# A new order of TensorE's attention part, and the half-used eighth pass of the third expert's layer 1 for four column blocks at once in 64-row halves

## The chip, the core and the metric

One core of a Trainium2 chip runs the kernel. The metric is the device time of one execution in microseconds (us). The engines of the core that appear below are TensorE (PE in the profile, its weight loads PEld), VectorE (DVE), ScalarE (ACT), GpSimd (POOL) and the DMA queue that SyncE issues (SP).

## The reference

Three layers in a row: an mLSTM attention (2 sequences, 8 heads, 768 tokens, head size 40), a dense mixture of 4 experts over the 1536 tokens of width 320, and a routed mixture of 8 experts of which each token takes one.

```python
# attention, per batch, head, token t
C = f_stab * C + i_stab * outer(v_t, k_t);  n = f_stab * n + i_stab * k_t
y_t = sigmoid(o_t) * (C @ q_t) / max(|n . q_t|, 1)
# first mixture: all 4 experts on all tokens, D = 320, F = 1024
out += p[:, e:e+1] * (relu(x @ w1[e]) @ w2[e])
# second mixture: expert = argmax(x @ w_gate); at most 384 tokens each
out[i] = gate_w[i] * (relu(x[i] @ w1[e]) @ w2[e])
```

The weights come as f32 and are used as pairs of f16 numbers (a high and a low part), so one f32 product is three f16 products.

## The kernel before

The attention is computed in 12 **units** of 128 tokens (2 sequences x 6 chunks). `front(u)` loads a unit, turns q and k by DMA transposes (line 1039), computes the scores (TensorE, line 1119, 8 matmuls), multiplies them by the decay mask on VectorE (line 1163, two halves), splits the product on ScalarE (line 1176) and GpSimd (line 1180) into a high and a low half, and `back(u)` uses both: TensorE's lines 1205 and 1210 (24 matmuls in the unit's second step), the update of the state (line 1273), then the output of the unit, which a DMA transpose (line 632) turns into `xT`, the input of the experts. `xT[:, t]` has five chunks of 128 rows for one tile of 128 tokens: width 320 is two and a half chunks, and chunk 2 holds the last 64 rows of the high part and the last 64 of the low part.

The experts are numbered 0 to 3 (first mixture) and 4 to 11 (second). Layer 1 of a tile (`tile_ops`) is two quads of four column blocks; each block takes 8 passes, listed in `L1_PAIRS` (line 635) as (high or low weights, chunk of the weights, chunk of `xT`). The last, (1, 2, 2), multiplies the low part of the weights' chunk 2 with `xT`'s chunk 2, where only the 64 high rows matter. A PSUM bank of a quad is evacuated by ScalarE (line 663, relu, high half) and VectorE (line 665, low half). Layer 2 of a tile is two halves of 12 matmuls (line 656); its bank is added to `acc` by VectorE (line 697).

Experts 0 and 1 run tile by tile between the attention's units. TensorE's order there is a table written by hand, `SEQ` (line 508): ("S", u) is the scores of unit u, ("B", u) its second part, ("L", k, t) layer 1 of expert k on tile t, ("M", k, t) its layer 2. Due times of all other engines and queues come from it: `Sched` lets every engine take the ready instruction whose result is due first. Where it estimates that TensorE would stand idle in the first part, it puts dummy matmuls (`warm`, line 416). Experts 2 and 3 run afterwards in groups of four tiles, 512 columns (`group_ops`, line 719). PSUM has eight banks; layer 1 takes them in turn from `hring` (there `ph0, ph1, x2, x1`), layer 2 from `oring` (there `po0, po1, x3, x0`).

Each weight matrix gets its scale from its largest magnitude: ScalarE and VectorE reduce it, GpSimd reduces over partitions (line 545), and a one-column matmul of TensorE spreads the scale over the partitions (line 551, a **spread**), placed in TensorE's order by `SPREAD_AT`. While the third expert runs, the weights of experts 8 to 11 and 4 are prepared in this way.

Of the kernel before, what the change touches and what calls it, by code (L numbers as in the profile page):

```python
# [10 lines left out]
F16 = mybir.dt.float16  # L11
# [238 lines left out]
def xlstm_moe_kernel(ctx: ExitStack, tc: tile.TileContext, a, cap: int):  # L250
# [467 lines left out]

    def group_ops(k, t0, nt, at, tail=None):
        wb, n = wbuf[at_work[k]], nt * 128  # L720
        for f in range(NF):
            kp = ps_tile("h")
            ph = bank[kp][:, 0:n]
            ph3 = ph.rearrange("p (t n) -> p t n", t=nt)
            add(
                "PE", 8 * n / 2400.0 + 0.02,
                lambda f=f, ph3=ph3: l1_mm(ph3, wb, f, lambda c: xT[:, t0:t0 + nt, c]),
                [("xT", t0 + j) for j in range(nt)] + w_keys(at_work[k], 1), [kp], at + 0.01 * f,
            )
            evac_ops(ph, kp, hb[0][:, f, 0:n], hb[1][:, f, 0:n], ("bh", f), ("bl", f), ["hbfree"])  # L730
# [1296 lines left out]
```

## Time and profile before

| | before |
|---|---|
| median of 3 runs, us | 496.05 (494.47 to 496.36) |
| profiled execution, us | 495.52 |
| its span in the profile, us | 493.8 |
| mean granted TensorE clock | 0.998 |
| PE, DVE, ACT, POOL busy, us | 475.5, 340.6, 311.9, 131.7 |
| first mixture and attention, third expert, fourth expert, second mixture, us from the span's start | 0 to 233.4, 233.4 to 312.8, 312.8 to 400, 400 to 493.8 |

The profile shows one execution. Busy time is what an engine worked; a matmul's shown end is modelled, so steps from one start to the next are more exact than durations. A wait is the idle time of an engine ahead of an instruction, with what ended it. TensorE's granted clock is written as a part of full speed.

### The profile page before, as it was taken

How to read it: one execution, taken by the hardware profiler on the slowest of the kernel's cores; microseconds unless marked ns; L12 is line 12 of the kernel's file. 1: busy time of each engine (PE TensorE's matmuls, PEld its weight loads, DVE VectorE, ACT ScalarE, POOL GpSimd, SP SyncE). 2: the span in 40 equal slices, each digit the busy share in tenths (PEclk: the TensorE clock that was granted, in tenths of full speed). 3: DMA queues.
4: the chain of work that ended last, by engine and by line, in shares of the span. 5: the costliest groups of instructions: out<-in, count | busy, mean ns of one | idle time of the engine just before them, and what ended most of it. 6: DMA issues, size and time to landing. Idle time of an engine off the chain costs nothing. (4 is left out here: it accounts for less than half of the span.)

```text
span 493.8 us, 13708 instructions
## 1 busy us (share of the span) xinstructions
PE 475.5 (96%) x5487; PEld 365.7 (74%) x5487; DVE 340.6 (69%) x972; ACT 311.9 (63%) x666; POOL 131.7 (27%) x243
## 2 busy tenths in 40 slices
PE   8999999999989899999999999999999999999994
PEld 6998978868868797886564746556564698888883
DVE  5898988799999834663968594879899982222120
ACT  1997979577687854856765568778879550322230
POOL 4751143665865410200010010000414111311111
PEclk9999999999999999999999999999999999999999
DMA  6996683354533796818686967628293545999200
GB/s 229 315 236 195 155 286 77 77 131 102 105 60 73 201 342 205 230 26 288 204 296 220 333 215 298 211 75 222 70 223 109 133 184 79 302 219 322 103 27 25
DMA packets 70772, 88.90 MB, mean 180 GB/s; under 512 B 48641, under 2 KB 56307, under 8 KB 70702
## 3 DMA queue, kind: packets, MB, share of 16 engines
q1 hardware_dynamic: 69502, 84.23, 59.4%
q0 software_dynamic: 1200, 3.73, 2.0%
q8 instruction: 45, 0.74, 0.6%
q14 instruction: 25, 0.20, 0.2%
HBM read 55.89 MB, written 21.70 MB: 157 GB/s over the span
## 5 line engine op out<-in xcount | busy, mean ns | idle before, releaser
L656 PEld LDWEIGHTS <-arena 128*128 128x128 f16 (+1 forms) x1416 | 136.4, 98 | 55.0 <-issue 3.2
L644 PEld LDWEIGHTS <-w 128*128 128x128 f16 x1792 | 97.3, 98 | 4.2 <-issue 2.8
L644 PE MATMUL ph<-xT,w 128*128 128x128 f16 (+3 forms) x1664 | 96.2, 217 | 1.2 <-DVE usm L442 0.9
L644 PEld LDWEIGHTS <-arena 128*128 128x128 f16 x960 | 64.2, 98 | 42.9 <-issue 1.8
L656 PE MATMUL po<-w,arena 128*128 128x320 f16 (+1 forms) x600 | 86.3, 299 | 2.1 <-DVE acc L697 1.3
L527 ACT ACTIVATE junk<-raw 128x512 bf16<-128x512 f32 (+1 forms) x105 | 69.6, 663 | 12.3 <-DMA raw<-in_moe_w_dram 10.8
L656 PE MATMUL po<-arena 128*128 128x320 f16 x504 | 71.3, 299 | 0.4 <-ACT arena L589 0.4
L665 DVE SCALAR_TENSOR_TENSOR arena<-ph,arena 128x512 f16<-128x512 f32 x80 | 54.5, 683 | 22.7 <-ACT arena L663 22.6
L644 PE MATMUL ph<-xT,arena 128*128 128x512 f16 (+4 forms) x512 | 66.7, 284 | 0.0
L589 ACT ACTIVATE w<-raw,wsm 128x640 f16<-128x640 f32 (+1 forms) x56 | 51.3, 961 | 18.1 <-DVE wsm L447 18.0
L663 ACT ACTIVATE arena<-ph 128x512 f16<-128x512 f32 x80 | 47.0, 587 | 22.7 <-PE ph L644 13.4
L594 DVE SCALAR_TENSOR_TENSOR w<-raw,wsm,w 128x640 f16<-128x640 f32 (+1 forms) x56 | 57.4, 1049 | 3.8 <-ACT w L589 3.7
L644 PE MATMUL x<-xT,arena 128*128 128x128 f16 (+4 forms) x448 | 52.2, 270 | 0.0
L545 POOL CROSS_LANE_REDUCE wsm<-wsm 128x1 f32<-128x6 f32 (+1 forms) x24 | 9.6, 402 | 107.9 <-ACT junk L527 78.7
L656 PE MATMUL x<-arena 128*128 128x320 f16 (+1 forms) x240 | 34.6, 299 | 0.1
L594 DVE SCALAR_TENSOR_TENSOR arena<-raw,wsm,arena 128x640 f16<-128x640 f32 (+1 forms) x28 | 30.4, 1103 | 3.0 <-ACT arena L589 3.0
L589 ACT ACTIVATE arena<-raw,wsm 128x640 f16<-128x640 f32 (+1 forms) x28 | 25.5, 955 | 3.6 <-DVE wsm L447 3.6
L685 POOL TENSOR_TENSOR cfs<-pw,invx 128x1 f32<-128x1 f32 x48 | 17.1, 388 | 37.1 <-DVE invx L452 29.8
L697 DVE SCALAR_TENSOR_TENSOR acc<-po,cfs,acc 128x320 f32<-128x320 f32 x30 | 16.4, 546 | 14.0 <-PE po L656 7.5
L1770 POOL DMA_INDIRECT out_dram<-acc,usm x13 | 12.7, 975 | 46.9 <-ACT acc L1767 45.0
L1180 POOL TENSOR_TENSOR arena<-arena 128x512 f16<-128x512 f32 x16 | 20.6, 1304 | 12.0 <-ACT arena L1176 12.0
L1457 POOL DMA_INDIRECT disp<-arena x12 | 13.8, 1150 | 34.5 <-ACT arena L663 17.3
(237 smaller groups left out, 649.3 us busy)
## 6 DMA issues: line engine op xcount, KB each, us to landing
raw<-in_moe_w_dram SPq DMA_DIRECT2D x36, 512.0 KB
raw<-in_moe_w_dram SPq DMA_DIRECT2D x24, 640.0 KB
ws<-w SPq DMA_DIRECT2D x8, 768.0 KB
ws<-w SPq DMA_DIRECT2D x8, 640.0 KB
arena<-in_att_dram SPq DMA_DIRECT2D x8, 492.0 KB
disp<-zero SPq DMA_DIRECT2D x1, 3936.0 KB
arena<-ws SPq DMA_DIRECT2D x4, 768.0 KB
arena<-ws SPq DMA_DIRECT2D x4, 640.0 KB
```

The lines of the kernel that those rows point to most:

```text
L527: nc.scalar.activation(out=junk[:, 0:w], in_=raw[:, i * w:(i + 1) * w], func=AF.Abs, accum_out=am[:, i:i + 1])
L589: lambda sl=sl: nc.scalar.activation(out=wh[:, sl], in_=raw[:, sl], func=AF.Copy, scale=sc),
L594: lambda sl=sl: nc.vector.scalar_tensor_tensor(wl[:, sl], raw[:, sl], sc, wh[:, sl], ALU.mult, ALU.subtract),
L644: nc.tensor.matmul(out=out, lhsT=wb[wi][:, c, f * 128:(f + 1) * 128], rhs=rhs(xc), start=(i == 0), stop=(i == LAST))
L656: nc.tensor.matmul(out=po[0:n, 0:DM], lhsT=hs[:, f, sl], rhs=ws[:, f, :], start=(f == 0 and i == 0), stop=(f == NF - 1 and i == 2),)
L663: act(0.52, lambda: nc.scalar.activation(out=hh, in_=ph, func=AF.Relu), [kp] + ex, [kh])
L665: 0.6, lambda: nc.vector.scalar_tensor_tensor(hl, ph, 0.0, hh, ALU.max, ALU.subtract),
L685: 0.26, lambda: nc.gpsimd.tensor_tensor(cf, pw[:, t, k:k + 1], invx[:, t:t + 1], ALU.mult),
L697: lambda: nc.vector.scalar_tensor_tensor(acc[:, t], po[:, 0:DM], cf, acc[:, t], ALU.mult, ALU.add),
L1180: 1.3, lambda j=j: nc.gpsimd.tensor_tensor(Wl[:, j::2], pb[:, j::2], Wh[:, j::2], ALU.subtract),
L1457: sent[k("done")] = nc.gpsimd.indirect_dma_start(out=disp_t[t], out_offset=bass.IndirectOffsetOnAxis(ap=sli, axis=0), in_=R.bitcast(U32), ...
L1770: nc.gpsimd.indirect_dma_start(out=view_of(), out_offset=bass.IndirectOffsetOnAxis(ap=ix[0:n], axis=0), in_=acc[0:n, y], in_offset=None, b ...
```

## The change

Two things, in one diff. First, another `SEQ`: the same items in another order. Second, the third expert's layer 1 (`group_ops` with `halves`) does 7 passes for each column block, and the eighth pass of four blocks together by `l1_halves_mm`: four matmuls of 64 rows, two on rows 0 to 63 with `xT`'s chunk 2 and two on rows 64 to 127 with `x4`, a copy of `xT`'s 64 high rows that three DMAs place there. The rows 64 to 127 of the weights' chunk 2 hold the same low part as the rows 0 to 63. The evacuations of the four blocks come after all of it, in the order 0, 2, 1, 3. The banks of the stage are dealt otherwise: six for layer 1 (`ph0, ph1, x2, x1, x3, x0`), two for layer 2 (`po0, po1`).

```diff
+    x4 = w2area.take([NT, 128], F16)
...
- ("S", 0), ("B", 0), ("S", 1), ("B", 1), ("L", 0, 0), ("S", 2), ("L", 0, 1), ("M", 0, 1), ("B", 2), ("S", 3), ("L", 0, 2),
+ ("S", 0), ("B", 0), ("S", 1), ("B", 1), ("L", 0, 0), ("L", 0, 1), ("S", 2), ("M", 0, 0), ("B", 2), ("L", 0, 2), ("S", 3),
...
-    def l1_mm(out, wb, f, rhs):
-        for i, (wi, c, xc) in enumerate(L1_PAIRS):
+    def l1_mm(out, wb, f, rhs, n=LAST + 1):
+        for i, (wi, c, xc) in enumerate(L1_PAIRS[:n]):
...
+    def l1_halves_mm(wb, q, out, t0, nt):
+        wi, c, xc = L1_PAIRS[LAST]
+        for y in range(2):
+            for z, x in enumerate((xT[0:64, t0:t0 + nt, xc], x4[64:128, t0:t0 + nt])):
+                f = q + 2 * z + y
+                nc.tensor.matmul(
+                    out=out[2 * z + y], lhsT=wb[wi][64 * z:64 * z + 64, c, f * 128:(f + 1) * 128], rhs=x,
+                    start=False, stop=True,
+                )
...
+            if halves:
+                add(
+                    "PE", 0.62, lambda q=q, ph3=ph3: l1_halves_mm(wb, q, ph3, t0, nt), keys + [("x4", t0)], kps,
+                    at + 0.01 * (q + 3) + 0.005,
+                )
+                for y in (0, 2, 1, 3):
+                    f = q + y
+                    evac_ops(phs[y], kps[y], hb[0][:, f, 0:n], hb[1][:, f, 0:n], ("bh", f), ("bl", f), ["hbfree"])
...
+    for t0 in range(0, NT, 4):
+        dma(
+            x4[64:128, t0:t0 + 4], xT[0:64, t0:t0 + 4, 2], 1.0, ["w2free"] + [("xT", t0 + j) for j in range(4)], [("x4", t0)],
+        )
...
     hring.append("x1")
-    oring.extend(["x3", "x0"])
+    hring.extend(["x3", "x0"])
     for t0 in range(0, NT, 4):
-        group_ops(2, t0, 4, at + 10 + 0.5 * t0)
-    hring.remove("x1")
-    del oring[2:]
+        group_ops(2, t0, 4, at + 10 + 0.5 * t0, None, True)
+    del hring[3:]
```

Counted over the whole program, the instructions differ in three places: 55 dummy matmuls instead of 64 (24 instead of 33 in the stretch from 16 us on), 24 matmuls of 64 rows in place of 24 of 128, and three DMAs more.

What the table does on VectorE can be counted in its order. The first mask multiply of units 4 to 11 stands at these places:

| unit | 4 | 5 | 6 | 7 | 8 | 9 | 10 | 11 |
|---|---|---|---|---|---|---|---|---|
| before | 155 | 198 | 234 | 258 | 296 | 315 | 349 | 373 |
| after | 133 | 171 | 202 | 256 | 288 | 318 | 353 | 369 |

Ahead of layer 1 of expert 0 on tile 3, VectorE's order has 157 instructions before and 190 after. TensorE's own order brings the scores of units 4, 5 and 6 by 7.8, 13.2 and 11.1 us of its work nearer to the start; those of units 7 to 11 move by 2.7 us or less.

**SP's queue**, where the tiles and units change places. Line 1039 (1065 after) is the transpose of a unit's q and k, line 632 (633) that of a unit's output into `xT`, line 422 (423) any other transfer. Before, from the transpose of tile 3 (first row):

```order
L632 DMA_TRANSPOSE xT<-arena 128x5x128
L1039 DMA_TRANSPOSE arena<-arena 128x16x128
L422 DMA arena<-in_att_dram 128x320
L422 DMA arena<-in_att_dram 128x984
L422 DMA arena<-arena 40x328 x2
L632 DMA_TRANSPOSE xT<-arena 128x5x128
L1039 DMA_TRANSPOSE arena<-arena 128x16x128
L422 DMA arena<-in_att_dram 128x984
L422 DMA arena<-in_att_dram 128x320
L1039 DMA_TRANSPOSE arena<-arena 128x16x128
L632 DMA_TRANSPOSE xT<-arena 128x5x128
```

and now, from the transpose of unit 5's q and k (first row):

```order
L1065 DMA_TRANSPOSE arena<-arena 128x16x128
L423 DMA arena<-in_att_dram 128x320
L423 DMA arena<-in_att_dram 128x984
L423 DMA gsm<-gsm 128x1x1
L633 DMA_TRANSPOSE xT<-arena 128x5x128
L423 DMA arena<-arena 40x328 x2
L423 DMA arena<-in_att_dram 128x320
L1065 DMA_TRANSPOSE arena<-arena 128x16x128
L423 DMA arena<-in_att_dram 128x984
L633 DMA_TRANSPOSE xT<-arena 128x5x128
L1065 DMA_TRANSPOSE arena<-arena 128x16x128
L633 DMA_TRANSPOSE xT<-arena 128x5x128
```

The transposes of units 5 and 6 now stand ahead of those of tiles 3 and 4, where they stood behind them; unit 7's stands ahead of tile 5's in both.

**TensorE at the end of a column block of the third expert** (`ph`, `x` and `po` are PSUM banks; `arena` holds weights and the copy `x4`). Before, from the last pass of one block, past the spread of a scale, to the first of the next:

```order
L644 MATMUL ph1_98<-xT_70,arena_88 128x512
L644 LDWEIGHTS arena_88
L644 MATMUL ph1_98<-xT_70,arena_88 128x512
L551 LDWEIGHTS call_68
L551 MATMUL x0_101<-wsm_82,call_68 128x1
```

and now, behind the seventh pass of the fourth block:

```order
L645 MATMUL x3_104<-xT_70,arena_88 128x512
L654 LDWEIGHTS arena_88
L654 MATMUL ph1_98<-xT_70,arena_88 128x512
L654 LDWEIGHTS arena_88
L654 MATMUL x1_102<-arena_88 128x512
L654 LDWEIGHTS arena_88
L654 MATMUL x2_103<-xT_70,arena_88 128x512
L654 LDWEIGHTS arena_88
L654 MATMUL x3_104<-arena_88 128x512
L645 LDWEIGHTS arena_88
L645 MATMUL x0_101<-xT_70,arena_88 128x512
```

Four half-row matmuls to four banks stand between the blocks, two of them with `xT` and two with the copy.

**TensorE at the spread of expert 11's second scale** (`call` is the matrix of ones). Before:

```order
L644 LDWEIGHTS arena_88
L644 MATMUL x2_103<-xT_70,arena_88 128x512
L551 LDWEIGHTS call_68
L551 MATMUL x3_104<-wsm_82,call_68 128x1
L644 LDWEIGHTS arena_88
L644 MATMUL x1_102<-xT_70,arena_88 128x512
```

and now:

```order
L667 LDWEIGHTS arena_88
L667 MATMUL po0_99<-arena_88 128x320
L552 LDWEIGHTS call_68
L552 MATMUL x3_104<-wsm_82,call_68 128x1
L645 LDWEIGHTS arena_88
L645 MATMUL ph0_97<-xT_70,arena_88 128x512
```

The spread stood behind two column blocks of layer 1 (lines 644) of its group; now it stands behind layer 2 of the group before (line 667) and ahead of the first block.

## Rows read from the trace of the kernel before

**Rows 1.** The page, part 1: busy time of each engine.

```profile
PE 475.5 (96%) x5487; PEld 365.7 (74%) x5487; DVE 340.6 (69%) x972; ACT 311.9 (63%) x666; POOL 131.7 (27%) x243
```

**Rows 2.** Windows: stretch, its length, then the engines' busy time, clock, DMA.

```profile
0.00:78.10 78.10, 74.62 (x858) 66.59 (x859) 65.25 (x175) 59.74 (x148) 34.36 (x81) 1.00 0.77 225
40.00:80.00 40.00, 38.53 (x531) 34.13 (x530) 34.28 (x97) 33.23 (x74) 12.53 (x31) 1.00 0.67 191
80.00:100.00 20.00, 19.89 (x291) 16.60 (x288) 16.90 (x55) 13.40 (x30) 8.47 (x17) 1.00 0.45 99
100.00:160.00 60.00, 56.01 (x896) 47.96 (x897) 58.08 (x153) 45.65 (x93) 39.41 (x51) 1.00 0.45 92
160.00:180.00 20.00, 18.73 (x217) 15.45 (x215) 12.82 (x24) 15.29 (x38) 6.49 (x10) 1.00 0.83 249
233.40:312.80 79.40, 77.62 (x474) 45.57 (x472) 59.05 (x107) 51.78 (x95) 5.01 (x12) 1.00 0.73 253
```

**Rows 3.** Waits of TensorE from 40 to 180 us: total, times, longest.

```profile
PE x L1119 <- DMA arena<-arena: 1.3, 2, 1.1
PE po L656 <- DVE acc L697: 1.3, 1, 1.3
PE x L1205 <- ACT arena L1176: 1.1, 1, 1.1
PE ph L644 <- DVE usm L442: 0.9, 1, 0.9
PE po L656 <- DVE arena L665: 0.8, 1, 0.8
```

**Rows 4.** Timeline of unit 7, 109 to 116 us: start, duration, instruction.

```profile
109.32 0.61 PE L1119 MATMUL x<-arena 120*128 120x128 f16 x8
...
111.40 3.74 PE L644 MATMUL ph<-xT,w 128*128 128x128 f16 x64
111.71 1.28 DVE L1163 TENSOR_TENSOR arena<-x,arena 128x512 f32<-128x512 f32 x2
...
112.48 1.23 ACT L1176 ACTIVATE arena<-arena 128x512 f16<-128x512 f32 x2 [0.42 <-DVE arena L1163]
...
113.19 2.65 POOL L1180 TENSOR_TENSOR arena<-arena 128x512 f16<-128x512 f32 x2 [1.08 <-ACT arena L1176]
...
115.19 0.51 PE L1210 MATMUL x<-arena 128*128 128x41 f16 x14
...
115.89 0.42 PE L1210 MATMUL x<-arena 128*128 128x41 f16 x10 [0.20 <-POOL arena L1180]
```

**Rows 5.** Instructions of line 416 from 16 to 45 us, by form.

```profile
L416 PE MATMUL ph<-zero x30: 269/272/282, 27.5 to 41.0; 128*128 128x256 f16 x30
L416 PE MATMUL x<-zero x3: 270/271/274, 16.7 to 16.9; 128*128 128x256 f16 x3
```

**Rows 6.** Timeline of TensorE around a pair of 24-row matmuls.

```profile
84.01 1.66 PE L656 MATMUL po<-w,arena 128*128 128x320 f16 x11
85.60 0.39 PE L1075 MATMUL x<-xT 24*128 24x512 bf16 x2
85.92 0.84 PE L644 MATMUL ph<-xT,w 128*128 128x128 f16 x12
```

**Rows 7.** Timeline of TensorE in the third expert.

```profile
245.44 1.79 PE L656 MATMUL x<-arena 128*128 128x320 f16 x12
247.07 1.79 PE L656 MATMUL po<-arena 128*128 128x320 f16 x12
...
258.60 1.89 PE L644 MATMUL x<-xT,arena 128*128 128x512 f16 x8
260.33 0.17 PE L551 MATMUL po<-wsm,call 128*128 128x1 bf16 x1
```

**Rows 8.** The page, part 5: evacuations of layer 1.

```profile
L665 DVE SCALAR_TENSOR_TENSOR arena<-ph,arena 128x512 f16<-128x512 f32 x80 | 54.5, 683 | 22.7 <-ACT arena L663 22.6
...
L663 ACT ACTIVATE arena<-ph 128x512 f16<-128x512 f32 x80 | 47.0, 587 | 22.7 <-PE ph L644 13.4
```

**Rows 9.** Timeline of TensorE at two spreads of a weight scale.

```profile
288.49 0.16 PE L551 MATMUL x<-wsm,call 128*128 128x1 bf16 x1 [1.07 <-POOL wsm L545]
288.52 1.89 PE L644 MATMUL x<-xT,arena 128*128 128x512 f16 x8
...
307.92 0.16 PE L551 MATMUL x<-wsm,call 128*128 128x1 bf16 x1 [0.71 <-POOL wsm L545]
```

More of the change, by code (lines that the diff above doesn't have):

```diff
@@ L508, in xlstm_moe_kernel @@
     SEQ = {x: i for i, x in enumerate((
- ("S", 0), ("B", 0), ("S", 1), ("B", 1), ("L", 0, 0), ("S", 2), ("L", 0, 1), ("M", 0, 1), ("B", 2), ("S", 3), ("L", 0, 2), ("B", 3), ("M", 0, 0), ("L", 1, 0), ("L", 1, 2), ("M", 1, 0), ("S", 4), ("M", 0, 2), ("L", 1, 1), ("B", 4), ("L", 0, 3), ("M", 1, 2), ("L", 1, 3), ("S", 5), ("L", 0, 4), ("S", 6), ("B", 5), ("M", 0, 4), ("L", 0, 5), ("S", 7), ("B", 6), ("M", 1, 1), ("L", 1, 5), ("B", 7), ("M", 0, 3), ("L", 1, 4), ("S", 8), ("B", 8), ("L", 0, 6), ("M", 0, 5), ("M", 1, 3), ("S", 9), ("B", 9), ("L", 0, 7), ("L", 0, 8), ("L", 1, 6), ("S", 10), ("M", 0, 7), ("L", 1, 9), ("M", 1, 6), ("M", 0, 8), ("M", 0, 6), ("L", 0, 10), ("B", 10), ("L", 0, 9), ("L", 1, 8), ("L", 1, 7), ("M", 0, 10), ("M", 1, 5), ("L", 1, 10), ("S", 11), ("M", 1, 8), ("M", 1, 4), ("B", 11), ("L", 0, 11), ("L", 1, 11), ("M", 1, 7), ("M", 0, 9), ("M", 1, 9), ("M", 1, 10), ("M", 1, 11), ("M", 0, 11),
+ ("S", 0), ("B", 0), ("S", 1), ("B", 1), ("L", 0, 0), ("L", 0, 1), ("S", 2), ("M", 0, 0), ("B", 2), ("L", 0, 2), ("S", 3), ("L", 1, 0), ("B", 3), ("S", 4), ("M", 0, 2), ("M", 1, 0), ("M", 0, 1), ("B", 4), ("L", 1, 1), ("S", 5), ("L", 1, 2), ("L", 1, 3), ("L", 0, 3), ("S", 6), ("B", 5), ("L", 0, 4), ("M", 1, 2), ("B", 6), ("M", 0, 3), ("L", 0, 5), ("M", 1, 1), ("M", 1, 3), ("S", 7), ("L", 1, 5), ("B", 7), ("S", 8), ("M", 0, 4), ("L", 1, 4), ("L", 0, 6), ("B", 8), ("M", 0, 5), ("L", 0, 7), ("S", 9), ("M", 0, 7), ("L", 0, 8), ("L", 1, 6), ("S", 10), ("L", 1, 9), ("M", 0, 6), ("L", 0, 10), ("L", 1, 8), ("L", 1, 7), ("L", 0, 9), ("L", 1, 10), ("M", 1, 7), ("B", 9), ("M", 1, 8), ("M", 1, 6), ("L", 0, 11), ("B", 10), ("M", 0, 9), ("L", 1, 11), ("M", 0, 8), ("M", 1, 5), ("M", 1, 10), ("S", 11), ("M", 1, 4), ("M", 1, 11), ("M", 0, 10), ("B", 11), ("M", 0, 11), ("M", 1, 9),
     ))}
@@ L717, in tile_ops, with group_ops @@
         l2_ops(k, t, wb, hh, hl, 0, [[("hh", i, g), ("hl", i, g)] for g in range(2)], at2)
-    def group_ops(k, t0, nt, at, tail=None):
+    def group_ops(k, t0, nt, at, tail=None, halves=False):
         wb, n = wbuf[at_work[k]], nt * 128
[L721 to L730, printed above, removed]
+        keys = [("xT", t0 + j) for j in range(nt)] + w_keys(at_work[k], 1)
+        for q in range(0, NF, 4):
+            kps, phs, ph3 = [], [], []
+            for f in range(q, q + 4):
+                kp = ps_tile("h")
+                ph = bank[kp][:, 0:n]
+                kps.append(kp)
+                phs.append(ph)
+                ph3.append(ph.rearrange("p (t n) -> p t n", t=nt))
+                passes = LAST if halves else LAST + 1
+                add(
+                    "PE", passes * n / 2400.0 + 0.02,
+                    lambda f=f, out=ph3[-1], passes=passes: l1_mm(out, wb, f, lambda c: xT[:, t0:t0 + nt, c], passes),
+                    keys, [kp], at + 0.01 * f,
+                )
+                if not halves:
+                    evac_ops(ph, kp, hb[0][:, f, 0:n], hb[1][:, f, 0:n], ("bh", f), ("bl", f), ["hbfree"])
+            if halves:
+                add(
+                    "PE", 0.62, lambda q=q, ph3=ph3: l1_halves_mm(wb, q, ph3, t0, nt), keys + [("x4", t0)], kps,
[4 more added lines that the diff above has]
+                    evac_ops(phs[y], kps[y], hb[0][:, f, 0:n], hb[1][:, f, 0:n], ("bh", f), ("bl", f), ["hbfree"])
         for j in range(nt):
@@ L1614, in xlstm_moe_kernel @@
     gate_weights()
+    for t0 in range(0, NT, 4):
+        dma(
+            x4[64:128, t0:t0 + 4], xT[0:64, t0:t0 + 4, 2], 1.0, ["w2free"] + [("xT", t0 + j) for j in range(4)], [("x4", t0)],
+        )
     for k in ORDER[4:]:
```

## The prediction

> **What bounds the kernel now.** I read the page's busy times first: TensorE works 475.5 us of a span of 493.8 us [rows 1], so the kernel is bound by TensorE's work nearly everywhere, and a change can gain in two ways only: less work on TensorE, or fewer of its waits. The windows say where the waits are [rows 2]: length less TensorE's busy time is 1.47 us in 40 to 80, 0.11 in 80 to 100, 3.99 in 100 to 160 and 1.27 in 160 to 180. In the dense stretch 100 to 160 VectorE works 58.08 of 60 us, while from 40 to 80 it is idle for 5.7 us and from 80 to 100 for 3.1. So in the second half of the attention VectorE is as much a bound as TensorE, and in the first half it has room. The waits of TensorE by releaser name VectorE at three of the five longest [rows 3], and a fourth (ScalarE's line 1176) stands right behind a VectorE multiply. The timeline of one unit shows the mechanism [rows 4]: unit 7's scores start at 109.32 and end at 109.93, VectorE takes up their mask multiply only at 111.71, 1.8 us later, because it is busy; ScalarE and GpSimd follow, and GpSimd's second half ends at 113.19 + 2.65 = 115.84. From the start of the scores that is 6.5 us, and TensorE, which had filled the time with a layer 1 (3.74 us) and other work, reaches that half at 115.69 and waits 0.20.
>
> The sum below is made against the profiled execution, 495.52 us (span 493.8). The median of the three runs is 496.05, 0.53 above it, and I add that at the end.
>
> **Dummies.** Nine dummy matmuls of 256 columns go, out of 33 between 16 and 45 us [rows 5]. A pass of 512 columns takes (260.33 - 258.60) / 8 = 0.216 us [rows 7], half of that is 0.108, so 9 x 0.108 = **-1.0 us**. They stand where TensorE is expected to wait for something, so the bounds are -1.0 and 0; I take -1.0, since TensorE's waits from 40 us on are small [rows 2] and real work (the second tile's layer 1) takes their place.
>
> **The new order.** Same work, so only waits can change. It brings the scores of units 4, 5 and 6 to the front by 8 to 13 us of TensorE's work, and with them 33 VectorE instructions ahead of layer 1 of expert 0 on tile 3. At the mean of 40 to 80, 34.28 / 97 = 0.35 us [rows 2], that is 11.7 us of VectorE's work. I work out what it meets. Before, TensorE reaches that layer 1 at 78.10 us, and VectorE has worked 65.25 us up to there, idle 12.85. Now TensorE has some 6.9 us more to do ahead of it (a layer 1 of 3.7 [rows 4], a layer 2 half of 1.63 [rows 7], scores, the second part of unit 4 and two small steps for 1.6 together) and 1.0 of dummies less, so it arrives at 84.0; VectorE has to have worked 76.9 by then. That leaves 7.1 us of idle time out of 12.85: 5.8 us of its idle time must be filled. There are 5.7 between 40 and 80 alone, though not all of it can be filled.
>
> What this buys lies later: the 3.99 us of waits in 100 to 160 belong to a VectorE that was 97% busy, and 11.7 us of its work have left the stretch or its queue. For units 6 to 10 I priced TensorE's new order from the start of the scores to the matmuls that read GpSimd's second half: 5.0, 4.9, 6.2, 5.2 and 5.3 us. The chain of unit 7 without its 1.8 us in VectorE's queue is 6.5 - 1.8 = 4.7 us [rows 4]. So all five just fit if VectorE takes up the scores at once, and none but unit 8 is near fitting if it does not. I take the 4.0 us as gone and 1.0 us of new waits ahead of tile 3's layer 1 as come: **-3.0 us**. Bounds: -5.3 (all that 100 to 180 holds) to +1.9 (first rival). SP's queue: the transposes of units 5 and 6 pass those of tiles 3 and 4, which delays each tile by one transpose; these tiles' layers 1 also stand later in TensorE's order (tile 3's by the 5.9 us above), which covers it, so 0.
>
> **The 64-row halves.** Removed: per group of four tiles and per four blocks, four passes of 0.216 = 0.864 us. Added: four half-row matmuls, in two pairs. The nearest rows are a pair of 24-row matmuls of 512 columns on different rows [rows 6]: layer 2's eleven from 84.01 step by 1.63 / 12 = 0.136 [rows 7], so they end at 85.50; the pair starts at 85.60 and the next matmul at 85.92. Its two matmuls of 0.216 each took one time 0.216, with about 0.10 us lost going in and 0.10 going out. So four matmuls cost 0.10 + 2 x 0.216 + 0.10 = 0.63 us against 0.864: -0.23, six times, **-1.4 us**. Bounds: +1.2 (no pair runs side by side: six times 0.20 of switching and nothing saved) to -2.6 (12 passes of 0.216 with no loss at the borders). The Trainium skill (TensorEngine Tiling (Array Packing), Theoretical Speedup) gives up to 2x for a contraction of at most 64 rows; by that alone it would be the -2.6. The same page (Key Properties) says that a change of the mode drains the engine, and the row's 0.10 us on either side agrees with that.
>
> The evacuations of four blocks now come in one burst. ScalarE takes 0.587 us for a block and VectorE 0.683 [rows 8], so a burst lasts 0.6 + 4 x 0.68 = 3.3 us. Behind it TensorE has two halves of layer 2 of the group before or the first half of its own (1.63 each [rows 7]) and a block of seven passes (1.51) ahead of the matmuls that need the last of the four: 4.8 us by the order. That covers 3.3 but not much more, as VectorE also reduces weights here (59.05 of 79.4 us [rows 2]): **+0.2 us**, between 0 and +3.
>
> The three copies into x4 need the tiles' `xT` and are read only after 233 us; they wait in SP's queue with nothing urgent behind them: 0. Layer 2 keeps two banks instead of four; a bank is free again after VectorE's addition of about half a microsecond, and the next tile's layer 2 takes 2 x 1.63 us: 0.
>
> **The spreads.** Before, TensorE waits 1.07 us for the scale of expert 11's second matrix at 288.49 and 0.71 for expert 4's at 307.92 [rows 9]. In the new order the first stands behind 36 matmuls of layer 2 since expert 11's first spread (4.9 us) where it stood behind 24 and two blocks (3.26 + 3.46 = 6.7): TensorE is there 1.8 us sooner, and the chain that makes the scale does not hang on that, so the wait grows to 2.9. From there to expert 4's spreads TensorE has 3.2 us more to do than before, so the wait of 0.71 goes. Net **+1.1 us**, bounds 0 and +1.8.
>
> **Sum.** -1.0 - 3.0 - 1.4 + 0.2 + 1.1 = -4.1: 495.5 - 4.1 = 491.4 for the profiled execution, 491.9 beside the median. With the nearer bounds of the terms beside the waits (dummies 0 to -1.0, halves -0.7 to -2.0, evacuations 0 to +1.0, spreads 0 to +1.8) this case runs from 491.9 - 0.6 - 0.2 - 1.1 = 490.0 to 491.9 + 1.0 + 0.7 + 0.8 + 0.7 = 495.1.
>
> **The rivals.** First, the waits only move. If VectorE still takes up the scores 1.8 us late in units 6 to 10, the shortfalls against 6.5 us are 1.5, 1.6, 0.3, 1.3 and 1.2, together 5.9 us in place of the 4.0: +1.9 where I put -3.0. Time: 491.9 + 4.9 = 496.8; with half of them, 494.5. For it: VectorE's total work is unchanged, and 58 of 60 us leave little room. Against: the work of units 4 to 6 starts sooner. Chance 0.24; it counts as no change.
>
> Second, slower: VectorE becomes the bound from about 60 us on. Its place is layer 1 of expert 0 on tile 3, whose input comes through VectorE. If none of the 12.85 us of idle time up to there can be filled (because VectorE there waits for loads and ScalarE), TensorE waits 5.8 us at about 84 us; with all of the 4.0 us of later waits gone that is 491.9 + 3.0 - 4.0 + 5.8 = 496.7, with all of them staying 500.7. It decides against the change from the point at which less than 2.2 of these 4.0 us go. Chance 0.12.
>
> Third, the half-row matmuls do not run side by side at 64 rows, or cost more at the borders: 491.9 + 2.6 = 494.5, chance 0.05. Fourth, the bursts stand open: 1 us in each of three groups, 494.7, and the Trainium skill (same page, PSUM Bottleneck) warns that tiling speeds up TensorE and not the evacuation. Chance 0.06. The change might also not do what it says if no wait and no pass were on the path; with TensorE at 96% that has hardly a chance.
>
> **How the numbers follow.** A measurement of this kernel can tell about 0.5%, 2.5 us, from no change. The forecast has 0.53. Faster (below 493.5) takes nearly all of it and a part of the third and fourth: 0.57. No change takes the first rival, what is left of the third and fourth, and the mildest part of the second: 0.31. Slower (above 498.5) is the second: 0.12. The range reaches from 488, where the waits give 2 us more of their bound of -5.3 beside the 490.0, to 498, which takes in the first rival whole and leaves out most of the second.
>
> **What would show it.** In the profile after: TensorE's waits in the stretch from 100 to 160 fall from 3.99 to about 1, and VectorE's busy time from 40 to 100 rises from 51.2 by some 6 us; a wait of more than 3 us at tile 3's layer 1 would be the second rival, waits of over 1 us at the lines 1210 of units 6, 7 and 9 the first. A block of the third expert takes 1.51 us and the four half-row matmuls 0.63 with their borders; 0.86 or more would refute that term. The wait for expert 11's second scale grows to 2 to 3 us, and that for expert 4's is gone. If the time comes out above 495, the step on the attention's waits is the one that failed.

## The result

| | before | after |
|---|---|---|
| median of 21 runs, us | 494.43 (490.32 to 497.12) | 498.29 (494.15 to 500.68) |
| ratio of the runs | | 1.0078, 95% interval 1.0060 to 1.0097 |
| profiled execution, us (span) | 495.52 (493.8) | 497.03 (495.3) |

The change is slower by 0.8%, some 3.9 us. I had forecast 4 us faster. Single executions of one kernel differ by up to 7 us, and the two profiled ones lie on the inner side of their medians, so the two traces differ by 1.5 us only; where it matters, below, further profiles of the changed kernel are read with the first.

TensorE's busy time is 1.2 us less than in [rows 1], on the page of the changed kernel:

```profile
PE 474.3 (96%) x5478; PEld 363.2 (73%) x5478; DVE 339.7 (69%) x972; ACT 312.2 (63%) x666; POOL 125.9 (25%) x243
```

The windows of the changed kernel (stretch, length, busy time of TensorE, its weight loads, VectorE, ScalarE, GpSimd, then clock and DMA), against [rows 2]:

```profile
40.00:80.00 40.00, 36.50 (x481) 31.16 (x480) 35.66 (x96) 32.83 (x70) 15.78 (x33) 0.96 0.75 193
80.00:100.00 20.00, 18.00 (x298) 15.71 (x296) 17.69 (x46) 14.96 (x35) 10.34 (x17) 1.00 0.45 95
100.00:160.00 60.00, 57.99 (x900) 49.57 (x897) 52.46 (x154) 42.79 (x91) 28.91 (x52) 1.00 0.40 80
160.00:180.00 20.00, 20.00 (x253) 17.03 (x249) 14.97 (x27) 17.42 (x37) 8.09 (x11) 1.00 0.69 194
233.40:312.80 79.40, 79.05 (x488) 44.77 (x487) 58.94 (x110) 51.95 (x97) 5.30 (x13) 1.00 0.74 259
```

Length less TensorE's busy time was 1.47, 0.11, 3.99 and 1.27 us; it is 3.50, 2.00, 2.01 and 0.00. So the waits from 100 to 160 us fell by 2.0 us, half of what I had put, and those from 160 to 180 by 1.3. But 3.9 us of new ones stand ahead of 100 us, and the granted clock from 40 to 80 us is 0.96 of full speed, where it was 1.00. VectorE worked 51.2 us from 40 to 100 and works 53.4: 2.2 us more, where I had looked for some 6. In the third expert (last row) TensorE's idle time fell from 1.78 to 0.35 us.

TensorE's waits from 40 to 180 us in the changed kernel, against [rows 3] (numbers: total, times, longest):

```profile
PE x L1145 <- DMA arena<-arena: 2.5, 2, 2.1
PE ph L645 <- DMA xT<-arena: 1.8, 2, 1.3
PE x L1299 <- DVE usm L448: 1.0, 1, 1.0
PE ph L645 <- DVE arena L676: 0.9, 1, 0.9
PE po L667 <- DVE arena L676: 0.7, 1, 0.7
```

The longest has a place: line 1145, the scores of unit 4 (line 1119 before). TensorE's timeline there:

```profile
59.37 1.79 PE L667 MATMUL po<-w,arena 128*128 128x320 f16 x12
63.23 0.62 PE L1145 MATMUL x<-arena 120*128 120x128 f16 x8 [2.06 <-DMA arena<-arena]
63.68 5.10 PE L667 MATMUL po<-w,arena 128*128 128x320 f16 x24
68.62 0.17 PE L1023 MATMUL x<-usm,call 128*128 128x4 bf16 x1
```

TensorE is done with the half of a layer 2 at 61.17 and waits 2.06 us for the transposed q and k of unit 4. Behind that the 24 matmuls of layer 2 take 68.62 - 63.68 = 4.94 us, where 24 take 2 x 1.63 = 3.26 at full speed [rows 7]. The windows of 2 us show why (column PEclk, the number ahead of the DMA share):

```profile
64.00:66.00 2.00, 2.00 (x9) 1.19 (x8) 1.75 (x3) 1.56 (x5) 1.44 (x2) 0.50 0.49 195
66.00:68.00 2.00, 2.00 (x12) 1.21 (x10) 0.00 (x0) 0.53 (x1) 0.07 (x1) 0.67 0.59 137
68.00:70.00 2.00, 2.00 (x32) 1.81 (x31) 1.15 (x7) 1.18 (x3) 0.06 (x1) 1.00 1.02 293
```

The clock goes from full speed (2.4 GHz) to 0.50 of it (1.2 GHz) and is back at 1.00 from 68 us on. Here is what the transposes waited for, in the timeline of all engines:

```profile
49.97 3.23 ACT L590 ACTIVATE w<-raw,wsm 128x1024 f16<-128x1024 f32 x3
...
54.31 0.82 ACT L1053 ACTIVATE arena<-arena,usm 128x640 f16<-128x640 f32 x1
...
55.42 1.00 DVE L1059 SCALAR_TENSOR_TENSOR arena<-arena,usm 128x320 f16<-128x320 f32 x2
...
56.49 3.44 SPq L1065 DMA_TRANSPOSE arena<-arena  x1
```

ScalarE first converts three pieces of expert 1's first weight matrix (line 590, 3.23 us), then scales unit 4's k and q (line 1053, the second at 54.31); VectorE takes the low parts (line 1059) until 56.42; the transposes are issued at 56.49 and the scores can start 6.7 us later. In the kernel before, the transposes and scores of unit 4 in the same view:

```profile
57.37 4.12 SPq L1039 DMA_TRANSPOSE arena<-arena  x1
...
69.55 0.61 PE L1119 MATMUL x<-arena 120*128 120x128 f16 x8
```

Transposes issued at 57.37, scores at 69.55: 12.2 us lay between. How much of that was room can be read where scores wait for their transposes, since the wait ends when these have landed. In the kernel before, unit 10's scores wait:

```profile
142.35 2.00 SPq L1039 DMA_TRANSPOSE arena<-arena  x1
...
148.40 0.62 PE L1119 MATMUL x<-arena 120*128 120x128 f16 x8 [1.11 <-DMA arena<-arena]
```

From issue to scores that is 6.05 us (3.7 at unit 6, the other unit that waits). So an estimate of unit 4's room from the trace before is 12.2 - 6.05 = 6.1 us, at most 8.5, and the new order moves its scores by 7.8 us of TensorE's work: there was little or none to spare. In the change the scores come 6.3 us sooner, their wait included, and the transposes that feed them 0.9.

In the third expert the halves came out as forecast and the spreads better. The half-row matmuls, in TensorE's timeline:

```profile
237.71 0.59 PE L645 MATMUL x<-xT,arena 128*128 128x512 f16 x2
238.24 0.39 PE L654 MATMUL ph<-xT,arena 64*128 64x512 f16 x1
238.24 0.39 PE L654 MATMUL x<-arena 64*128 64x512 f16 x1
238.47 0.38 PE L654 MATMUL x<-xT,arena 64*128 64x512 f16 x1
238.47 0.38 PE L654 MATMUL x<-arena 64*128 64x512 f16 x1
238.78 0.39 PE L645 MATMUL x<-xT,arena 128*128 128x512 f16 x1
```

The last full pass of the block starts at 237.93 (the first of the two at 237.71, 0.216 later), the halves at 238.24 and 238.47, the next full pass at 238.78: both matmuls of a pair start together, and the group costs 238.78 - 237.93 - 0.216 = 0.63 us in place of 0.864. TensorE reaches the two spreads of [rows 9] at these times and waits at neither:

```profile
286.78 0.17 PE L552 MATMUL x<-wsm,call 128*128 128x1 bf16 x1
...
309.01 0.17 PE L552 MATMUL x<-wsm,call 128*128 128x1 bf16 x1
```

In the second mixture the trace shows waits that the kernel before had not, 2.2 us in all from 400 to 450 us. The longest, with "issue" for time in which the engine waited for nothing that the profile shows:

```profile
PE po L1833 <- issue: 0.8, 1, 0.8
```

### The profile page after: what moved, and what is told of

It is laid out like the page before. It is cut to its first block, busy times and chain, and to the rows that moved or that the text cites. A ratio compares the mean times of both kernels' runs of the same rounds, so it can differ in the third digit from the quotient of the medians.

```text
span 495.3 us, 13706 instructions
## 1 busy us (share of the span) xinstructions
PE 474.3 (96%) x5478; PEld 363.2 (73%) x5478; DVE 339.7 (69%) x972; ACT 312.2 (63%) x666; POOL 125.9 (25%) x243
## 5 line engine op out<-in xcount | busy, mean ns | idle before, releaser
L645 PEld LDWEIGHTS <-arena 128*128 128x128 f16 x936 | 61.5, 98 | 40.8 <-issue 3.9
L667 PE MATMUL po<-arena 128*128 128x320 f16 x648 | 90.5, 299 | 0.1
L667 PE MATMUL po<-w,arena 128*128 128x320 f16 (+1 forms) x600 | 88.7, 303 | 0.7 <-DVE arena L676 0.7
L676 DVE SCALAR_TENSOR_TENSOR arena<-ph,arena 128x512 f16<-128x512 f32 x76 | 51.6, 683 | 20.4 <-ACT arena L674 20.3
L674 ACT ACTIVATE arena<-ph 128x512 f16<-128x512 f32 x76 | 44.5, 589 | 26.4 <-PE ph L645 12.3
L645 PE MATMUL ph<-xT,arena 128*128 128x128 f16 (+4 forms) x472 | 57.8, 275 | 0.7 <-DMA xT<-disp 0.7
L645 PE MATMUL x<-xT,arena 128*128 128x128 f16 (+4 forms) x464 | 56.5, 274 | 0.7 <-issue 0.5
L708 DVE SCALAR_TENSOR_TENSOR acc<-po,cfs,acc 128x320 f32<-128x320 f32 x36 | 19.6, 544 | 14.0 <-PE po L667 6.8
L1206 POOL TENSOR_TENSOR arena<-arena 128x512 f16<-128x512 f32 x16 | 20.7, 1310 | 17.7 <-ACT arena L1202 17.6
L1793 DVE SCALAR_TENSOR_TENSOR arena<-ph,arena 128x512 f16<-128x512 f32 (+1 forms) x10 | 6.5, 651 | 24.2 <-ACT arena L1788 24.2
L1793 DVE SCALAR_TENSOR_TENSOR arena<-x,arena 128x512 f16<-128x512 f32 (+1 forms) x10 | 6.5, 652 | 23.9 <-ACT arena L1788 23.9
```

The costliest lines, as they stand in the source:

```text
L645: nc.tensor.matmul(out=out, lhsT=wb[wi][:, c, f * 128:(f + 1) * 128], rhs=rhs(xc), start=(i == 0), stop=(i == LAST))
L667: nc.tensor.matmul(out=po[0:n, 0:DM], lhsT=hs[:, f, sl], rhs=ws[:, f, :], start=(f == 0 and i == 0), stop=(f == NF - 1 and i == 2),)
L674: act(0.52, lambda: nc.scalar.activation(out=hh, in_=ph, func=AF.Relu), [kp] + ex, [kh])
L676: 0.6, lambda: nc.vector.scalar_tensor_tensor(hl, ph, 0.0, hh, ALU.max, ALU.subtract),
L708: lambda: nc.vector.scalar_tensor_tensor(acc[:, t], po[:, 0:DM], cf, acc[:, t], ALU.mult, ALU.add),
L1206: 1.3, lambda j=j: nc.gpsimd.tensor_tensor(Wl[:, j::2], pb[:, j::2], Wh[:, j::2], ALU.subtract),
```

## The experiments

All ratios are to the kernel before on the same chip, with 95% intervals. Four groups of four ran, each on one chip: (seq_only, halves_only, s4_later, rep), (s4_dummies, s4_two, old_then_new, new_then_old), (turn_early, rep_b, s4_two_b, halves_b), (amx_early, turn_amx, s4_dummies_b, rep_c). Theory A is what the trace above suggests: the scores of unit 4 stand too early in the new order, ahead of their transposes. Theory B: the halves, their copies or the banks cost the time. Theory C: VectorE is the bound up to 100 us, wherever the scores stand. A theory D comes up further below.

**seq_only: only the new order.** The kernel before with the new `SEQ` line.

> Only the new order of the attention part; the third expert as before. Theory A (the order makes unit 4's scores reach TensorE before their transposed q and k have landed; TensorE waits about 2 us and then runs at half clock for some 3 us, 3.8 us in all, and the halves gain about 2): slower than before by about 5.5 us, ratio near 1.011, with the half-clock stretch near 64 us. Theory B (the loss comes from the halves, their copies or the other banks): ratio 1.000 or below.

Ratio 1.0063 (1.0030 to 1.0096), 3.1 us slower, where I had expected 5.5. The wait (2.09 us) and a clock of 0.50 from 64 to 66 us are there. The order alone carries most of the loss; theory B falls.

**halves_only and halves_b: only the halves.** The changed kernel with the old `SEQ` line, run twice.

> Only the 64-row halves, the copies and the other banks; the order of the attention part as before. Theory A: faster than before by about 2 us, ratio near 0.996, and no stretch at half clock in the attention part. Theory B: slower, ratio 1.006 or above.

> Only the halves, again. Their trace showed six times 0.634 us in place of 0.864, and both waits at the spreads gone, against bursts of evacuations of up to 0.8 us: about 2 us less in the third expert. If that reaches the end of the program: ratio 0.995 to 0.998. If it is given back further on: 0.999 to 1.002.

Ratios 0.9998 (0.9971 to 1.0025) and 1.0008 (0.9983 to 1.0032): no change. The halves cost 0.63 us in these traces too and the waits at the two spreads are gone, which is 3.2 us by the two terms; but little more than 1 us, if anything, reaches the end, where I had expected 2. A part is given back in the stage itself. From the start of the third expert's stage (at 233.42 us in the kernel before) to the fourth expert's first layer 2 the kernel before takes 93.25 us, halves_only 91.71 and halves_b 92.56. TensorE waits there for evacuations of layer 1, 0.26 and 0.66 us in halves_only and 0.26 in halves_b, and in halves_b for the addition (line 708) that frees one of the two banks left to layer 2:

```profile
PE po L667 <- DVE acc L708: 1.5, 1, 1.5
```

Whether the 0.7 to 1.5 us that are left reach the end, the two runs cannot tell.

**s4_later: one exchange.**

```diff
- ("B", 3), ("S", 4), ("M", 0, 2), ("M", 1, 0),
+ ("B", 3), ("M", 0, 2), ("S", 4), ("M", 1, 0),
```

> The change with one exchange in its table: the scores of unit 4 behind the layer 2 of expert 0 on tile 2 instead of ahead of it (3.3 us later). Theory A: the wait of 2 us and the half clock behind it go, about 3.8 us faster than the change, ratio near 1.000 to the kernel before. Theory C (VectorE is the bound up to 100 us, so what TensorE does not wait there it waits further on): as the change, ratio near 1.008, with the wait moved to a layer 1 or a second part between 70 and 100 us. Theory B: ratio near 1.008 too, with the wait gone.

**rep, rep_b, rep_c: the change again.**

> The change once more, unaltered, for a second profile of it. Theory A: the wait ahead of unit 4's scores and the granted clock of about 0.5 behind it come again, at the same place within 1 us. If the wait or the clock is an accident of one execution they are missing here, and the ratio stays near 1.008 all the same.

> The change a third time, beside the others on one chip. Theory A: ratio 1.007 to 1.011, the wait of about 2 us at unit 4's scores and the half clock again. Its second mixture tells whether the 2 us lost there in the two profiles of the change so far come again.

> The change once more, as the neighbour of the run with dummies. Ratio 1.006 to 1.010.

One exchange of two neighbours in a table of 72 takes the ratio from 1.0104 (1.0066 to 1.0142, rep) to 1.0021 (0.9987 to 1.0055) on one chip: 3.3 us between the medians. The wait at unit 4's scores is gone, and so is the half clock behind it. Yet TensorE's idle time from 40 to 80 us is still 3.20 us (3.50 in the first profile of the change), now for VectorE at a layer 2, at unit 4's second part and at a layer 1, as theory C had it; what fell is the idle time from 80 to 160 us, from 4.0 to 1.1. This profile is the fastest of the run's executions, 4.9 us below their median. The change itself repeats as 1.0104, 1.0070 and 1.0071, with the wait at 1.92, 1.98 and 2.21 us. But the half clock does not repeat: rep has it, rep_b and rep_c do not. In rep_c, the first of the windows above:

```profile
64.00:66.00 2.00, 2.00 (x17) 1.46 (x15) 1.75 (x3) 1.95 (x6) 1.51 (x2) 1.00 0.46 178
```

and TensorE's timeline (unit 4's scores, the layer 2 behind them, and the second part of layer 2 of expert 1 on tile 2):

```profile
63.14 0.62 PE L1145 MATMUL x<-arena 120*128 120x128 f16 x8 [2.21 <-DMA arena<-arena]
63.59 3.42 PE L667 MATMUL po<-w,arena 128*128 128x320 f16 x24
66.86 0.17 PE L1023 MATMUL x<-usm,call 128*128 128x4 bf16 x1
...
83.15 1.53 PE L667 MATMUL po<-w,arena 128*128 128x320 f16 x10 [2.07 <-DVE arena L676]
```

The layer 2 behind the scores now takes 66.86 - 63.59 = 3.27 us, at full speed. What was saved there is waited for later: the last row waits 2.07 us, where the first profile of the change had 0.72. From the start of the scores to that last row it is 20.0 us in rep_c, 20.6 in rep_b (no half clock either), and 20.3 and 21.1 in the two profiles of the change with the half clock. Two other kernels with the same order there had it too: 22.4 us in seq_only, 20.7 in new_then_old (below).

**s4_dummies and s4_dummies_b: the wait filled.** Nineteen dummies of 256 columns right ahead of unit 4's scores.

```diff
         def scores():
+            for _ in range(19 if u == 4 else 0):
+                nc.tensor.matmul(
+                    out=bank["x0"][:, 0:256], lhsT=zero16[:, 0:128], rhs=zero16[:, 0:256], start=True, stop=True
+                )
             for h in range(H):
```

> The change with 19 dummy matmuls of 256 columns (19 x 0.108 = 2.05 us) right ahead of unit 4's scores, into the bank that the scores then overwrite; order otherwise unaltered. If TensorE's idle time ahead of these scores is what the half clock follows: the scores start where they did (the wait is filled, not shortened), the granted clock behind them stays at 1.00, the 24 matmuls of layer 2 behind them take 3.4 us in place of 5.1, and the time is 1.5 to 2 us below the change's, ratio to before about 1.005. If the clock falls for another reason: the scores come up to 0.3 us later, the clock still reads 0.5 behind them, and the time is the change's, 1.008 to 1.010.

> The change with 19 dummies ahead of unit 4's scores again. If the half clock costs time by itself: 1.5 us or more below the run of the change beside it. If the wait at layer 2 of expert 1 on tile 2 takes it back (VectorE is late whatever TensorE's clock): within 1 us of it, with that wait at 2 to 2.8 us.

Ratios 1.0007 (0.9975 to 1.0040) and 1.0031 (0.9997 to 1.0066), the second 1.0 us below its neighbour rep_c by medians. The clock stayed at 1.00 behind the scores in both profiles, but fell behind a later wait (see the last section). In the second:

```profile
62.73 2.24 PE L1145 MATMUL x<-zero 128*128 128x256 f16 x19
64.98 0.62 PE L1149 MATMUL x<-arena 120*128 120x128 f16 x8
65.44 3.42 PE L667 MATMUL po<-w,arena 128*128 128x320 f16 x24
...
86.08 2.85 PE L667 MATMUL po<-w,arena 128*128 128x320 f16 x10 [3.15 <-DVE arena L676]
```

The dummies fill the wait, the layer 2 runs at full speed, and the wait of 3.15 us at 86.08 takes it back: 21.1 us from the scores to that row (20.3 in s4_dummies). That is the second expectation of s4_dummies_b, with a wait still longer than the 2 to 2.8 us expected. So the traces show no clear cost of the half clock: 20.3 to 22.4 us with it behind the scores, 20.0 to 21.1 without. The times leave more open. The interval of s4_dummies lies below those of the change in the first result, rep and rep_c and just reaches that of rep_b; that of s4_dummies_b overlaps with its neighbour's; and the profile of s4_dummies is the slowest of its executions. A gain of up to some 3 us from filling the wait is not excluded.

**s4_two and s4_two_b: two places further back in the table.**

```diff
- ("B", 3), ("S", 4), ("M", 0, 2), ("M", 1, 0), ("M", 0, 1), ("B", 4), ("L", 1, 1), ("S", 5),
+ ("B", 3), ("M", 0, 2), ("M", 1, 0), ("S", 4), ("M", 0, 1), ("L", 1, 1), ("B", 4), ("S", 5),
```

> The change with the scores of unit 4 two layers 2 later (6.5 us of TensorE's work) and its second part behind layer 1 of expert 1 on tile 1. Theory A (scores ahead of their transposes are the whole loss): wait and half clock gone, as in the run with one exchange, ratio 0.998 to 1.002. Theory C (VectorE is the bound to 100 us): the waits at the second part of unit 4, layer 2 of expert 1 on tile 2 and layer 1 of expert 0 on tile 3 stay or grow to 4 us or more together, ratio 1.004 or above.

> The change with the scores of unit 4 two layers 2 later, again, on the chip of the run of the change beside it: 3.5 to 5.5 us below it by theory A; less than 2 us if the earlier difference was one of chips. Ratio to before 0.996 to 1.001.

Ratios 0.9988 (0.9968 to 1.0009) and 0.9978 (0.9948 to 1.0008), the second 5.2 us below rep_b on one chip. The planner did not follow the table all the way: in the traces the scores stand behind 12 matmuls of layer 2 more than in the change, 1.6 us of work and not the 6.5 expected (in s4_later behind 24 more). The half clock is gone, and of the wait of some 2 us at unit 4's scores 0.48 and 0.86 us are left, about what 1.6 us leave. The times are theory A's, not theory C's, though waits of 1.8 us at the second part of unit 4 and 1.3 us at a layer 1 came up between 70 and 82 us: from 40 to 80 us TensorE idles 2.80 and 3.55 us, as in the change, and the gain lies behind that.

**old_then_new and new_then_old: the table in halves.** Both tables hold the same items in their first 27 places, so they can be cut there.

> The change with the first 27 places of its table as before (both tables hold the same 27 items there) and the new order behind them. Theory A, and the loss only in the first part: ratio 0.994 to 0.999, since the new second part has fewer of the waits of 100 to 160 us (theirs were 4 us before). If the new order gains nothing in the second part either: 1.000 to 1.003.

> The reverse: the new order in the first 27 places, the old one behind. Theory A: the wait of 2 us ahead of unit 4's scores and the half clock are there, ratio 1.008 to 1.012. If the loss needs the new second part: 1.003 or below.

Ratios 0.9995 (0.9959 to 1.0030) and 1.0232 (1.0191 to 1.0272). With the old first part the new second part neither gains nor loses, which misses the first expectation: TensorE's idle time from 100 to 160 us is 3.62 us there (before 3.99). With the new first part the old second part costs another 1.3% or more on top of the change, over the range that I had expected. The waits of TensorE of that kernel from 40 to 180 us begin with:

```profile
PE x L1145 <- DMA arena<-arena: 5.1, 4, 2.2
```

Scores wait for their transposes four times, unit 4's with 2.2 us among them. So the change's loss comes in with the first 27 places, and the gain after 100 us comes only where both parts of the new table stand together.

**turn_early: the transposes, not the scores.** Table as in the change; only the planner's urgency of unit 4's load, scaling and transposes is raised (and set back behind them).

```diff
-        sch.ahead = 0.0
+        sch.ahead = 8.0 if u == 4 else 0.0
...
+            sch.ahead = 0.0
```

> The change with only the urgency of unit 4's load, scaling and transposes raised (8 us in the planner), the table as in the change: ScalarE scales unit 4's q and k ahead of the conversion of expert 1's first matrix. If the scores of unit 4 wait because this chain stands behind that conversion: the wait of 2 us falls below 0.5 us with no half clock behind it, and layer 1 of expert 1 on tile 0 waits instead, up to 2 us, for its weights; ratio to before 1.000 to 1.006, at least 1 us below the change on this chip. If the transposes are late for another reason (their own time in the queue): wait and half clock stay, ratio 1.008 to 1.010.

Ratio 0.9981 (0.9948 to 1.0014), 5.7 us below rep_b on one chip, and faster than the bound that I had set. In the timeline of all engines the two steps on ScalarE have changed places:

```profile
50.05 1.55 ACT L1053 ACTIVATE arena<-arena,usm 128x640 f16<-128x640 f32 x2
...
53.03 2.01 SPq L1065 DMA_TRANSPOSE arena<-arena  x1
...
53.09 3.21 ACT L590 ACTIVATE w<-raw,wsm 128x1024 f16<-128x1024 f32 x3
...
63.30 0.61 PE L1146 MATMUL x<-arena 120*128 120x128 f16 x8
```

The scaling (line 1053) stands at 50.05, ahead of the conversion at 53.09; the transposes are issued 3.5 us earlier and the scores at 63.30 wait for nothing. The same 576 matmuls (dummies left out) stand ahead of them as in the change. The weights came in time as well. That the scores start no sooner than in the change (63.23) is this execution's clock, which fell to 0.50 at 36 to 38 us; in rep, where it did too, they start at 64.78. The edit moved more than the two steps, since the planner places everything else anew: the layer 1 of expert 1 on tile 0, whose weights are converted later, now stands right ahead of the scores, where in the change a half of a layer 2 stood between. Its windows:

```profile
40.00:80.00 40.00, 39.05 (x542) 34.56 (x540) 37.93 (x110) 34.75 (x75) 17.18 (x34) 1.00 0.81 192
80.00:100.00 20.00, 19.05 (x295) 16.54 (x293) 16.44 (x55) 17.17 (x41) 6.45 (x12) 1.00 0.40 106
100.00:160.00 60.00, 59.06 (x922) 50.75 (x921) 54.88 (x147) 43.83 (x90) 34.11 (x59) 1.00 0.43 81
```

Idle time of TensorE: 0.95, 0.95 and 0.94 us, in place of 3.50, 2.00 and 2.01 in the change, and 1.47, 0.11 and 3.99 before. From 40 to 180 us that is 2.84 us in place of 6.84 before: the table gains the waits that I had forecast once unit 4's input is there.

One mark takes in the whole attention part, the start of the third expert's stage, at 233.4 us before [rows 2]. It is at 231.0 and 234.3 in the two runs with the old table and the halves, at 235.1, 237.2, 234.4 and 235.4 in the four profiles of the change, at 229.8 in turn_early, 230.2 in s4_later, and 230.4 and 231.2 in s4_two and s4_two_b.

**amx_early and turn_amx: the way on.** What makes 2 us of wait cost 4 and more? In rep_c, VectorE's timeline and SP's queue read as a chain:

```profile
67.09 0.16 DVE L443 TENSOR_SCALAR usm<-x 128x4 uint32<-128x4 uint32 x1 [1.28 <-PE x L1023]
...
72.48 0.53 DVE L1059 SCALAR_TENSOR_TENSOR arena<-arena,usm 128x320 f16<-128x320 f32 x1
...
81.32 1.18 DVE L998 TENSOR_REDUCE usm<-arena 128x3 f32<-128x984 f32 x1 [2.19 <-DMA arena<-in_att_dram]
...
82.41 0.68 DVE L676 SCALAR_TENSOR_TENSOR arena<-ph,arena 128x512 f16<-128x512 f32 x1
```

```profile
73.04 1.84 SPq L1065 DMA_TRANSPOSE arena<-arena  x1
74.98 1.62 SPq L423 DMA_DIRECT2D arena<-in_att_dram  x2
```

A one-column matmul (line 1023) that spreads unit 5's scales stands behind unit 4's scores on TensorE; VectorE waits 1.28 us for it at 67.09. Its scaling of unit 5 ends at 73.01, unit 5's transposes are issued at 73.04, and in SP's queue the load of a later unit stands behind them (74.98). VectorE's next reduction needs that load and waits 2.19 us until 81.32, and queued behind that reduction is the evacuation (line 676, 82.41) for which layer 2 of expert 1 on tile 2 waits. Theory D is that this chain makes the later wait, so that an earlier matmul of unit 5's scales opens it. Two kernels try that, on the change and on turn_early:

```diff
-  ["x3"], SEQ["B", u - 1] - 0.5,
+  ["x3"], SEQ["S", 4] + 0.05 if u == 5 else SEQ["B", u - 1] - 0.5,
```

> The change with the one-column matmul of unit 5's scales right behind unit 4's scores, 4.9 us of TensorE's work earlier (the planner moves other engines' work with it; the load of unit 6 then stands ahead of unit 5's transposes in SP's queue). Theory D (the wait at layer 2 of expert 1 on tile 2, 0.7 to 2.8 us so far, comes from VectorE waiting for unit 6's load, which stands behind unit 5's transposes): the wait ahead of unit 4's scores stays near 2 us or falls a little, VectorE's wait for a load between 76 and 84 us falls below 0.5 us, the layer 2's wait below 0.5 us, ratio 1.000 to 1.005. If that wait has another cause: it stays above 0.7 us, ratio 1.007 to 1.010.

> Both: unit 4's transposes earlier and unit 5's matmul of scales earlier. Theory D: no wait over 0.5 us at unit 4's scores, less waiting than in the run with the transposes alone, ratio 0.994 to 0.998, which would be faster than before. If the scales are not what holds unit 5: as with the transposes alone, 0.997 to 0.999.

amx_early: 1.0006 (0.9977 to 1.0036), 2.8 us below rep_c by medians. The time is theory D's, but its trace does not show the mechanism: VectorE's wait for the load is 1.9 us, not below 0.5, and other evacuations are waited for instead, since the planner moved much else; the profiled execution, 497.71 us, also lies 3.9 us above the run's median. So the chain stays open. But unit 4's scores still wait 2.12 us there, with the half clock behind them, and the loss is nearly gone: that wait alone does not set the time. turn_amx: 0.9955 (0.9923 to 0.9987), a median of 490.62 against 493.28: faster than the kernel before, and 5.9 us below the change beside it, with no wait at unit 4's scores (62.25). Against turn_early, on another chip, the intervals overlap, so what the second edit adds is open.

## Why the prediction was wrong

- **The waits of the attention part: the step that failed.** I put the waits from 100 to 160 us at -4.0 and new ones ahead of tile 3's layer 1 at +1.0. The first was right in sign and half the size: -2.0 in the first profile of the change (with another -1.3 from 160 to 180, which the sum had only in its bound). The second was wrong by its place and size: +3.9 ahead of 100 us, and 1.7 of half clock beside it; TensorE came to tile 3's layer 1 at 89.0, not at 84.0. The step set TensorE ("it arrives at 84.0") against VectorE ("has to have worked 76.9 by then"), and asked of the early scores only whether VectorE would be free behind them. It never asked whether their own input would be there. The numbers were at hand in the trace before: 12.2 us from issue to scores at unit 4, 6.05 and 3.7 at the two units whose scores wait. I had computed that unit 4's scores come 7.8 us of TensorE's work sooner, and I showed SP's queue for units 5 and 6, but not that unit 4's transposes stayed where they were. In four profiles of the change TensorE's idle time from 40 to 180 us is 7.5 to 9.1 us (before 6.84), with a further 1.7 of half clock in the two lower ones: 2 to 3 us more than before, where I had put 3 less. That the loss starts at unit 4's scores is shown by turn_early, s4_later and s4_two_b: each takes away most or all of their wait, in its own way, and each comes out 3.3 to 5.7 us below the change on its chip. How a wait of 2 us becomes a loss of 4 and more is not shown: the waits behind it, to 160 us, go with it, but the one edit at the chain that might link them (amx_early) took most of the loss and left both that wait and the one for the load standing.
- **The second rival** had a wait at the right stretch, but in the wrong place: it wanted VectorE late at tile 3's layer 1. That wait came (0.9 us); the one that mattered came some 27 us sooner, at a DMA.
- **Dummies, -1.0:** the nine are gone, and TensorE's idle time from 0 to 40 us is 2.90 us, where it was 2.01. So about -0.1 is left, if that idle time belongs to them; the bound of 0 was the better choice.
- **The halves, -1.4:** right to a hundredth by the trace, 6 x (0.864 - 0.634) = 1.4, with pairs that start together. The third rival falls. That halves_only and halves_b gained nothing in time is explained in part, by the waits that came up in the same stage.
- **The spreads, +1.1:** wrong in sign. TensorE came to expert 11's second scale 4.91 us behind the first, as worked out, but did not wait at all. I had said that the chain that makes the scale "does not hang on that"; but the scale came sooner too. VectorE's last reduction of the weights, which waits for their load in both kernels, started at 285.52 before and at 284.29 in the change, though the stage began 1.7 us later, and GpSimd's step behind it took 0.33 us where it had taken 1.31. Why the load came sooner is open. This wait was gone in all 16 profiles of kernels with the halves.
- **The bursts, +0.2:** single waits for an evacuation of 0.28 us at 295.44 and 0.91 us at 214.89, where a tile's layer 1 comes between the third expert's blocks. Some 1 us, within the bounds.
- **Two banks for layer 2, 0:** too low. TensorE waited for the addition that frees a bank (line 708) 1.1 to 1.6 us in seven of those 16 profiles and 0.4 to 0.9 in four more, though not in the first of the change, nor in before and seq_only, which have four banks there.
- **Not in the sum:** the second mixture. Between 400 and 450 us TensorE waited 2.2 us in the first profile of the change (0.8 of it at line 1833, 0.7 for gathered rows), 2.6 and 2.2 in rep and rep_b, 0.9 in rep_c, and 0.2 in the kernel before. s4_later had 0.5. Whether it belongs to the order or to chance in the executions stays open.

## What to carry to other kernels

When work is moved forward on one engine, ask for every moved instruction when its inputs land in the trace of before, and by how much the instruction that feeds it moves; the time between a transfer's issue and its reader, less what a like transfer takes to a reader that waits for it, is the room, and a move beyond it turns into a wait. If the feeder sits behind work that is not urgent, moving the feeder forward can be worth more than moving the reader back: turn_early kept the new table and came out 5.7 us below the change, s4_later 3.3 and s4_two_b 5.2. A wait need not cost its own length: count who stands behind the waiting instruction on each of the engines. That is advice from the reading of one trace; the edit aimed at the chain did not confirm it.

## What the runs showed of the hardware that I had not expected

TensorE's granted clock fell to 0.50 behind an idle time of 2.06 us ahead of unit 4's scores (also 1.92 in rep, 2.09 in seq_only, 2.12 in amx_early and 2.21 in new_then_old), but not behind 1.98 us in rep_b and 2.21 in rep_c at the same place. At the later layer 2 it fell behind 2.30 us in s4_dummies and 3.15 in s4_dummies_b (the ten matmuls at 86.08 above took 2.85 us, in seq_only 1.53), but not behind 2.66 in rep_b and 2.80 in seq_only. So the length of the wait does not tell in these runs. Nor is the fall tied to the new order: it came at 50 to 54 us in halves_b too. And where it came behind the scores, the way to the next long wait, which VectorE sets, was not clearly longer than without it.

A pair of 64-row matmuls of 512 columns starts within 5 ns, and the next pair 0.23 us later, little more than one full pass (0.216). The pair of 24-row matmuls before also starts within 4 ns. Going in and out of the mode cost 0.096 and 0.09 us, in all six groups of the change and in every other kernel with the halves.
